# Gate and up weights in two pieces each, and a down projection that writes output rows directly, at the end of a memory-bound decode kernel

## The chip, the cores and the metric

The kernel runs on one core of one Trainium2 chip. The metric is the device time of one execution in microseconds (us); I quote medians of several runs. In the profile, PE is the tensor engine's matmuls, PEld its weight loads, DVE the vector engine, ACT the scalar engine, SP the engine that issues the large DMAs, and PEclk the tensor engine's granted clock as a share of full speed. "L748" is a line of that kernel's source; the same statement has other line numbers in other kernels.

## The reference, cut to what matters

Four sequences, one new token each (B = 4, model width D = 512): attention over a cache of 8192 keys for 32 heads, then a gated feed-forward block (F = 1792).

```
h   = x + attention(layernorm(x), k_cache, v_cache, wq, wo)
n   = layernorm(h)
g   = n @ w_gate                 # [4, 512] @ [512, 1792]
u   = n @ w_up                   # [4, 512] @ [512, 1792]
out = h + (sigmoid(g) * u) @ w_down     # [4, 1792] @ [1792, 512]
```

The two caches are 537 MB in bfloat16; the three weights of the feed-forward block are 1.8 MB each.

## The kernel before

The caches stream through a ring of four buffers for some 1250 us. The change touches only what follows: the loads of the last weights, and the feed-forward block. There, `NFT = 14` tiles of F, `NDC = 4` chunks of D. Activations are kept transposed (the feature on the 128 partitions, 4 columns for the batch), so each weight block of 128 x 128 is the stationary operand and only 4 columns are streamed through it:

```
WD_PARTS = [(0, 7), (7, 12), (12, NFT)]      # w_down arrives in three pieces
...
def pe_gu(e, wv, bk):                        # gate, then up
    mm = None
    for t in range(NFT):
        for c in range(NDC):
            mm = e.matmul(bk[:, B * t:B * t + B], wv[:, c, t:F:NFT],
                          hnT[:, B * c:B * c + B], start=(c == 0), stop=(c == NDC - 1))
    return mm
p_g = P("pe", lambda e: pe_gu(e, wg_v, bS[0]), [d_hn, dma_of[("wg", 0)][0]])
p_u = P("pe", lambda e: pe_gu(e, wu_v, bS[1]), [dma_of[("wu", 0)][0]])
a_sig = ...                                  # sg_sb = sigmoid(gate)
d_hh = ...                                   # hh_sb = sg_sb * up
...
        for c in range(NDC):                 # down, for t in the piece
            mm = e.matmul(bH[:, B * c:B * c + B], wd_v[:, t, 128 * c:128 * (c + 1)],
                          hh_sb[:, B * t:B * t + B], ...)
...
d_o = ...                                    # oT = h + down, rearranged to (b c) columns
p_o = P("pe", lambda e: e.matmul(bP[0][0:NB, 0:128], oT[:, :], ident[:, :], ...), ...)   # transpose
o0 = P("dve", lambda e: e.tensor_copy(o_sb[:, :], bP[0][0:NB, 0:128]), [p_o])
# then one DMA to out
```

In the first argument of `P` stands the engine, in the last list what the operation waits for.

## Time and profile before

| | before |
|---|---|
| time, median of 6 runs | 1287.07 us (1286.68 to 1287.3) |
| profiled span | 1285.0 us |
| moved from HBM | 550.77 MB at 429 GB/s |
| chain that ended last | 84% DMA |

These are lines of the page of the kernel before (busy tenths in 40 slices; then HBM traffic; then the chain that ended last, by engine).

```profile
DMA  9999999999999999999999999999999999999998
HBM read 550.77 MB, written 0.00 MB: 429 GB/s over the span
DMA 84%; PE 13%; DVE 2%; issue 0%; SPq 0%; DVEq 0%
```

The DMA engines are busy from first to last. This change moves no byte less and does not touch the loads of the caches, so the time before the last weights arrive should stay as it is; only what happens between the last landings and the end can move. So this is the timeline of the end, with the columns: start, duration, engine, line, operation, output<-inputs, shapes, count, and in brackets how long the engine was idle just before and what ended that.

```profile
1267.83 1.44 PE L715 MATMUL PS<-A_sb,kT 128*128 128x4 bf16 x48 [0.22 <-DMA kT<-in_A_wo_dram]
...
1271.48 0.17 DVE L739 TENSOR_TENSOR hnT<-hc,tst 128x16 bf16<-128x16 f32 x1
...
1272.49 3.49 PE L748 MATMUL PS<-hnT,ring 128*128 128x4 bf16 x56 [2.11 <-DMA ring<-in_B_w_gate_dram]
1276.83 3.52 PE L748 MATMUL PS<-hnT,ring 128*128 128x4 bf16 x56 [0.85 <-DMA ring<-in_B_w_up_dram]
1280.46 0.21 DVE L754 TENSOR_TENSOR hh_sb<-sg_sb,PS 128x56 bf16<-128x56 f32 x1 [8.80 <-PE PS L748]
...
1280.73 1.66 PE L762 MATMUL PS<-hh_sb,ring 128*128 128x4 bf16 x56 [0.38 <-DVE hh_sb L754]
1282.42 0.19 DVE L768 TENSOR_TENSOR oT<-h,PS 128x16 bf16<-128x16 f32 x1 [1.75 <-PE PS L762]
...
1282.67 0.28 PE L771 MATMUL PS<-ident,oT 128*16 128x128 bf16 x1 [0.28 <-DVE oT L768]
1282.98 0.28 DVE L773 CAST o_sb<-PS 16x128 bf16<-16x128 f32 x1 [0.37 <-PE PS L771]
```

Three things are to be seen. Gate waits for its whole weight, although its input was ready 0.8 us sooner, and up waits 0.85 us for its own. A gate or up matmul takes 63 ns (3.52 us / 56), a down matmul only 29.6 ns (1.66 us / 56), both at the same granted clock of 0.50, as the windows view says (the down stretch; its limits and length, then busy time and number of instructions of PE, PEld, DVE, ACT and POOL, then PEclk, the DMA share and GB/s):

```profile
1280.73:1282.39 1.66, 1.65 (x56) 1.56 (x56) 0.00 (x0) 0.00 (x0) 0.00 (x0) 0.50 0.00 0
```

And after down there are three more steps, with hand-offs between engines, before the output DMA.

The last weight pieces land close behind. From the DMA issues of the same kernel (KB, median us from issue to landing; the issues started at 1244.6, 1263.4 and 1265.3) the three pieces of the down weight land at about 1279.0, 1280.5 and 1281.2:

```profile
ring<-in_B_w_down_dram SPq DMA_DIRECT2D x1, 896.0 KB, 34.3
ring<-in_B_w_down_dram SPq DMA_DIRECT2D x1, 640.0 KB, 17.1
ring<-in_B_w_down_dram SPq DMA_DIRECT2D x1, 256.0 KB, 15.9
```

### The profile page before, as it was taken

To read this page: it belongs to the slowest core of one execution; us is meant where nothing else is said; L and a number is where in the kernel's file an instruction comes from. 1 tells how busy PE (TensorE), PEld (TensorE's weight loads), DVE (VectorE), ACT (ScalarE), POOL (GpSimd) and SP (SyncE) were. 2 spreads that over 40 slices of the span, in tenths; PEclk is the share of its full clock that TensorE was granted. 3 is DMA by queue.
4 is the path that set the end of the run, shared out by engine and by line. 5 is a ranking of instruction groups with operands and counts; after the bars stand their busy time and mean duration, and the time that the engine had idled before them with its cause. 6 is when DMAs were issued, how large, how long until landed. Compare 5 with 4: busy or idle time off the path is not lost.

```text
span 1285.0 us, 11783 instructions
## 1 busy us (share of the span) xinstructions
PE 499.6 (39%) x4851; PEld 187.0 (15%) x4851; DVE 634.8 (49%) x659; ACT 77.2 (6%) x150; POOL 8.3 (1%) x23
## 2 busy tenths in 40 slices
PE   3434344334244244333434343253342442343445
PEld 1011111111011011111111111010110111111114
DVE  4974634635545545535536445445445446355300
ACT  2010100001010010100101000010100101000011
POOL 2000000000000000000000000000000000000000
PEclk9995565565665665565665665655665656655665
DMA  9999999999999999999999999999999999999998
GB/s 406 429 431 430 433 431 432 431 432 433 429 432 432 430 431 431 432 431 433 430 433 430 432 431 430 433 429 435 429 435 429 436 428 432 432 429 433 430 435 341
DMA packets 20405, 550.95 MB, mean 429 GB/s; under 512 B 2212, under 2 KB 2216, under 8 KB 3624
## 3 DMA queue, kind: packets, MB, share of 16 engines
q1 hardware_dynamic: 20384, 550.78, 99.7%
q8 instruction: 8, 0.13, 0.0%
q14 instruction: 5, 0.04, 0.0%
q10 hardware_dynamic: 8, 0.00, 0.0%
HBM read 550.77 MB, written 0.00 MB: 429 GB/s over the span
## 4 chain that ended last, share of the span: by engine, by line
DMA 84%; PE 13%; DVE 2%; issue 0%; SPq 0%; DVEq 0%
DMA ring<-in_A_v_cache_dram 79%; PE PS L544 8%; PE PS L522 4%; DMA ring<-in_B_w_up_dram 3%; DMA ring<-in_A_k_cache_dram 2%; DVE kT L497 1%; DMA ring<-in_A_wq_dram 1%; PE PS L575 1%; PE PS L427 0%; PE PS L748 0%; DVE Lq L470 0%; DVE ring L444 0%; PE PS L454 0%; PE PS L762 0%; SPq L325 0%
## 5 line engine op out<-in xcount | busy, mean ns | idle before, releaser
L497 DVE STREAM_TRANSPOSE kT<-ring 128x1024 uint32<-128x1024 uint32 x512 | 588.4, 1209 | 475.1 <-DMA ring<-in_A_k_cache_dram 474.9
L522 PE MATMUL PS<-kT,Lqg 128*32 128x512 bf16 x2048 | 242.2, 621 | 569.4 <-DVE kT L497 569.4
L544 PE MATMUL PS<-ring,PTz 128*32 128x512 bf16 x2048 | 216.1, 568 | 192.1 <-DMA ring<-in_A_v_cache_dram 192.1
L522 PEld LDWEIGHTS PS<-kT,Lqg 128*32 128x32 bf16 x2048 | 69.5, 135 | 700.5 <-DVE kT L497 445.5
L544 PEld LDWEIGHTS PS<-ring,PTz 128*32 128x32 bf16 x2048 | 64.6, 128 | 311.6 <-DMA ring<-in_A_v_cache_dram 183.3
L606 DVE STREAM_TRANSPOSE Et<-Ep 128x512 bf16<-128x512 bf16 x16 | 11.4, 712 | 96.4 <-ACT Ep L601 96.4
L579 ACT ACTIVATE negm<-PS 128x1 f32<-128x1 f32 x16 | 2.7, 171 | 669.3 <-PE PS L575 669.3
L616 ACT ACTIVATE PTz<-Et 64x512 bf16<-64x512 bf16 x32 | 34.0, 1062 | 13.6 <-DVE Et L606 13.2
L645 ACT ACTIVATE A_sb<-PS 32x32 bf16<-32x32 f32 x16 | 3.7, 231 | 479.5 <-PE PS L643 479.5
L621 DVE TENSOR_SCALAR Zs<-PS,rinv 128x512 f32<-128x512 f32 x16 | 11.6, 723 | 27.6 <-PE PS L544 27.6
L629 PE MATMUL PS<-SelZ,Zs 128*128 128x8 f32 x128 | 18.6, 272 | 0.9 <-DVE Zs L621 0.9
L629 PEld LDWEIGHTS PS<-SelZ,Zs 128*128 128x128 f32 x128 | 17.1, 208 | 10.6 <-issue 10.6
L558 DVE TENSOR_REDUCE mx<-PS 128x1 f32<-128x512 f32 x16 | 10.5, 657 | 4.2 <-PE PS L522 4.2
L581 ACT ACTIVATE E_sb<-PS,negm 128x512 bf16<-128x512 f32 x16 | 11.0, 688 | 0.7 <-ACT negm L579 0.3
L601 ACT ACTIVATE Ep<-PS 128x512 bf16<-128x512 f32 x16 | 9.6, 597 | 11.1 <-PE PS L597 11.1
L586 PEld LDWEIGHTS PS<-sig,Gsum 128*128 128x128 f32 x32 | 7.8, 305 | 13.1 <-issue 13.1
L586 PE MATMUL PS<-sig,Gsum 128*128 128x1 f32 x32 | 9.2, 356 | 0.0
L575 PEld LDWEIGHTS PS<-onesf,rowx 1*128 1x128 f32 x32 | 6.9, 267 | 12.8 <-issue 12.8
L444 DVE CAST ring<-PS 128x512 bf16<-128x512 f32 x4 | 2.5, 683 | 12.2 <-PE PS L427 12.2
L575 PE MATMUL PS<-onesf,rowx 1*128 1x1 f32 x32 | 8.2, 324 | 0.0
L748 PE MATMUL PS<-hnT,ring 128*128 128x4 bf16 x112 | 7.0, 199 | 3.0 <-DMA ring<-in_B_w_gate_dram 2.1
L635 DVE TENSOR_TENSOR OD<-PS,SelD 128x32 bf16<-128x32 f32 x16 | 2.5, 157 | 10.3 <-PE PS L629 10.3
(87 smaller groups left out, 98.2 us busy)
## 6 DMA issues: line engine op xcount, KB each, us to landing
ring<-in_A_k_cache_dram SPq DMA_DIRECT2D x64, 4096.0 KB, 29.5
ring<-in_A_v_cache_dram SPq DMA_DIRECT2D x64, 4096.0 KB, 33.6
ring<-in_A_wq_dram SPq DMA_DIRECT2D x1, 4096.0 KB, 12.5
kT<-in_A_wo_dram SPq DMA_DIRECT2D x1, 2560.0 KB, 21.4
ring<-in_B_w_gate_dram SPq DMA_DIRECT2D x1, 1792.0 KB, 28.7
ring<-in_B_w_up_dram SPq DMA_DIRECT2D x1, 1792.0 KB, 32.7
kT<-in_A_wo_dram SPq DMA_DIRECT2D x1, 1536.0 KB, 24.6
ring<-in_B_w_down_dram SPq DMA_DIRECT2D x1, 896.0 KB, 34.3
```

Source lines behind the costliest of these rows:

```text
L497: return e.transpose(kT[:, buf, i * q:(i + 1) * q].bitcast(U32), ringv(src)[:, base + i * q:base + (i + 1) * q].bitcast(U32))
L522: mm = e.matmul(bS[g % 2][32 * j:32 * (j + 1), :], Lqg[:, g % 2, l0:l0 + 32], rhs, start=(s % GS == 0 and v == 0), stop=(s % GS == GS - 1 ...
L544: mm = e.matmul(bO[g % 2][32 * rq:32 * (rq + 1), :], PTz[:, g % 2, l0:l0 + 32], ringv(slot)[:, r0 * 128:(r0 + 4) * 128], start=(s % GS == ...
L558: mx_of[g] = P("dve", lambda e: e.tensor_reduce(mx[:, :], bS[g % 2][:, :], AX.X, ALU.max), [sc_of[g * GS + GS - 1], p1_of.get(g - 1)], kin ...
L575: p2_of[g] = P("pe", lambda e: e.matmul(bX[:, 0:1], rowx[0:1, :], onesf[0:1, 0:1], start=True, stop=True), [d2b_of[g], c_ones], kind="p2")
L581: exp_of[g] = P("act", lambda e: e.activation(E_sb[:, :], bS[g % 2][:, :], ACT.Exp, bias=negm[:, 0:1], scale=SCALE, accum_out=sig[:, 0:1]) ...
L586: L_of[g] = P("pe", lambda e: e.matmul(bX[:, 0:1], Gsum[:, :], sig[:, 0:1], start=True, stop=True), [exp_of[g], a1_of[g], d_g], kind="L")
L601: epc_of[g] = P("act", lambda e: e.activation(Ep[:, :], bP[0][:, :], ACT.Copy), [pt_of[g], et_of.get(g - 1)], kind="epc")
L606: et_of[g] = P("dve", lambda e: e.transpose(Et[:, :], Ep[:, :]), [epc_of[g]] + list(ptc_of.get(g - 1, ())), kind="et")
L616: return e.activation(dst, src, ACT.Copy)
L621: z_of[g] = P("dve", lambda e: e.tensor_scalar(Zs[:, :], bO[g % 2][:, :], rinv[:, g % 2:g % 2 + 1], None, op0=ALU.mult), [pv_of[g * GS + G ...
L629: mm = e.matmul(bP[1][:, 0:8], Zs[:, 128 * r:128 * (r + 1)], SelZ[:, r, :], start=(r == 0), stop=(r == 3))
```

## The change

Its intent: let gate and up start on the first half of their weights, and let the down projection leave its result in the layout of the output, so that the residual add and the transposing matmul after it fall away. The core of the diff (the split of the two loads, with a semaphore for each half, and the zeroing of `hhz` are cut):

```diff
-        def pe_gu(e, wv, bk):
+        def pe_gu(e, wv, bk, i):
             mm = None
-            for t in range(NFT):
-                for c in range(NDC):
-                    mm = e.matmul(bk[:, B * t:B * t + B], wv[:, c, t:F:NFT],
-                                  hnT[:, B * c:B * c + B], start=(c == 0), stop=(c == NDC - 1))
+            for c in range(2 * i, 2 * i + 2):
+                for t in range(NFT):
+                    mm = e.matmul(bk[:, B * t:B * t + B], wv[:, c, t:F:NFT], hnT[:, B * c:B * c + B],
+                                  start=(c == 0 and t == 0), stop=(c == NDC - 1 and t == NFT - 1), ...)
             return mm
 ...
-        d_hh = ...(hh_sb[:, :], sg_sb[:, :], bS[1][:, 0:NFT * B], ALU.mult)
+        d_hh = ...(hhz[:, :, 3:3 + NB:4], sg_sb ..., bS[1] ..., ALU.mult)
 ...
+        o_ps = bP[0][0:NB, 0:128]
+        p_h = P("pe", lambda e: e.matmul(o_ps, hb[:, :], identf[:, :], start=True, stop=False, ...), ...)
 ...
-                        mm = e.matmul(bH[:, B * c:B * c + B], wd_v[:, t, 128 * c:128 * (c + 1)],
-                                      hh_sb[:, B * t:B * t + B], ...)
+                        mm = e.matmul(o_ps, hhz[:, t, 3 - c:3 - c + NB], wd_v[:, t, 128 * c:128 * (c + 1)],
+                                      start=False, ...)
 ...
-        d_o = ...      # residual add
-        p_o = ...      # transposing matmul
-        o0 = P("dve", lambda e: e.tensor_copy(o_sb[:, :], bP[0][0:NB, 0:128]), [p_o])
+        o0 = P("dve", lambda e: e.tensor_copy(o_sb[:, :], o_ps), [p_d[-1]])
```

How the shifted slices work: for each tile `t`, `hhz` has 20 columns, all zero but columns 3, 7, 11 and 15, which hold the four sequences. The slice of 16 columns that starts at `3 - c` has sequence b in its column 4b + c. With it as the stationary operand and a down block as the streamed one, the product lands in output row 4b + c, which is where chunk c of sequence b belongs; the other 12 rows get zero added. The roles have swapped: 16 columns are loaded, and the 128 columns of the weight are streamed. `p_h` starts the sum with the residual.

More of the change, by code (lines that the diff above doesn't have):

```diff
@@ L246, in bass_sequential_preLN__mha_block_cached__glu_gated_glu__decode_kernel @@
         hc = SB("hc", [128, NDC * B], FP32)
+        hb = SB("hb", [128, NDC * B], FP32)
         hnT = SB("hnT", [128, NDC * B], BF16)
         sg_sb = SB("sg_sb", [128, NFT * B], FP32)
-        hh_sb = SB("hh_sb", [128, NFT * B], BF16)
-        oT = SB("oT", [128, B * NDC], BF16)
+        hhz = SB("hhz", [128, NFT, 20], BF16)
         o_sb = SB("o_sb", [B * NDC, 128], BF16)
@@ L267, in bass_sequential_preLN__mha_block_cached__glu_gated_glu__decode_kernel @@
         s_slot = [SEM(f"s_slot{i}") for i in range(NS)]
-        s_piece = [SEM(f"s_piece{i}") for i in range(7)]
+        s_piece = [SEM(f"s_piece{i}") for i in range(9)]
         def ringv(slot):
@@ L333, in f @@
                                            B_w_down.rearrange("(p t) f -> p t f", p=128)[:, t0:t1, :]
-                                           ).then_inc(s_piece[3 + i], 16)
-                    ops.append((f, s_piece[3 + i], 16))
-                return ops
-            if kind == "wu":
-                sem, val = s_piece[6], 16
-            else:
-                uses[slot] += 1
-                sem, val = s_slot[slot], 16 * uses[slot]
+                                           ).then_inc(s_piece[2 + i], 16)
+                    ops.append((f, s_piece[2 + i], 16))
+                return ops
+            if kind in ("wg", "wu"):
+                ops = []
+                for i in range(2):
+                    wv, src, sem = (wg_v, B_w_gate, s_piece[5 + i]) if kind == "wg" else (wu_v, B_w_up, s_piece[7 + i])
+                    def f(e, i=i, wv=wv, src=src, sem=sem):
+                        return e.dma_start(wv[:, 2 * i:2 * i + 2, :],
+                                           src.rearrange("(c p) f -> p c f", p=128)[:, 2 * i:2 * i + 2, :]).then_inc(sem, 16)
+                    ops.append((f, sem, 16))
+                return ops
+            uses[slot] += 1
+            sem, val = s_slot[slot], 16 * uses[slot]
             if kind == "k":
@@ L345, in load @@
                 dst, src = ringv(slot), kv_src(t, A_v_cache)
-            elif kind == "wq":
+            else:
                 dst, src = wq_v, A_wq.rearrange("(p c) f -> p c f", p=128)
-            elif kind == "wg":
-                dst, src = wg_v, B_w_gate.rearrange("(c p) f -> p c f", p=128)
-            else:
-                dst, src = wu_v, B_w_up.rearrange("(c p) f -> p c f", p=128)
             return [(lambda e: e.dma_start(dst, src).then_inc(sem, 16), sem, val)]
@@ L382, in bass_sequential_preLN__mha_block_cached__glu_gated_glu__decode_kernel @@
                        [zs4])
+        zhh = pool(lambda e: e.memset(hhz[:, :, :], 0.0))
         zif = pool(lambda e: e.memset(identf[:, :], 0.0))
@@ L741, in bass_sequential_preLN__mha_block_cached__glu_gated_glu__decode_kernel @@
                                                   mean_b(20), ALU.mult), [d_rs, d_hc])
+        d_hb = P("dve", lambda e: e.tensor_copy(hb[:, :].rearrange("p (b c) -> p c b", c=NDC),
+                                                h2[:, 0, :].rearrange("p (c b) -> p c b", c=NDC)), [d_h])
         P("act", lambda e: e.activation(lnst[0:B, 10:11], tst[0:B, 12:13], ACT.Sigmoid), [a_sq])
-        def pe_gu(e, wv, bk):
+        def pe_gu(e, wv, bk, i):
             mm = None
-            for t in range(NFT):
-                for c in range(NDC):
-                    mm = e.matmul(bk[:, B * t:B * t + B], wv[:, c, t:F:NFT],
-                                  hnT[:, B * c:B * c + B], start=(c == 0), stop=(c == NDC - 1))
-            return mm
-        p_g = P("pe", lambda e: pe_gu(e, wg_v, bS[0]), [d_hn, dma_of[("wg", 0)][0]])
-        p_u = P("pe", lambda e: pe_gu(e, wu_v, bS[1]), [dma_of[("wu", 0)][0]])
-        a_sig = P("act", lambda e: e.activation(sg_sb[:, :], bS[0][:, 0:NFT * B], ACT.Sigmoid), [p_g])
-        d_hh = P("dve", lambda e: e.tensor_tensor(hh_sb[:, :], sg_sb[:, :], bS[1][:, 0:NFT * B], ALU.mult), [a_sig, p_u])
+            for c in range(2 * i, 2 * i + 2):
+                for t in range(NFT):
+                    mm = e.matmul(bk[:, B * t:B * t + B], wv[:, c, t:F:NFT], hnT[:, B * c:B * c + B],
+                                  start=(c == 0 and t == 0), stop=(c == NDC - 1 and t == NFT - 1), skip_group_check=True)
+            return mm
+        p_g, p_u = [], []
+        for ps, kind, wv, bk in ((p_g, "wg", wg_v, bS[0]), (p_u, "wu", wu_v, bS[1])):
+            for i in range(2):
+                ps.append(P("pe", lambda e, wv=wv, bk=bk, i=i: pe_gu(e, wv, bk, i), [d_hn, dma_of[(kind, 0)][i]]))
+        a_sig = P("act", lambda e: e.activation(sg_sb[:, :], bS[0][:, 0:NFT * B], ACT.Sigmoid), [p_g[1]])
+        d_hh = P("dve", lambda e: e.tensor_tensor(hhz[:, :, 3:3 + NB:4], sg_sb[:, :].rearrange("p (t b) -> p t b", b=B),
+                                                  bS[1][:, 0:NFT * B].rearrange("p (t b) -> p t b", b=B), ALU.mult),
+                 [a_sig, p_u[1], zhh])
+        o_ps = bP[0][0:NB, 0:128]
+        p_h = P("pe", lambda e: e.matmul(o_ps, hb[:, :], identf[:, :], start=True, stop=False, skip_group_check=True),
+                [d_hb, c_identf, epc_of[gl]])
         p_d = []
@@ L761, in pe_down @@
                     for c in range(NDC):
-                        mm = e.matmul(bH[:, B * c:B * c + B], wd_v[:, t, 128 * c:128 * (c + 1)],
-                                      hh_sb[:, B * t:B * t + B], start=(t == 0 and c == 0),
-                                      stop=(t == NFT - 1 and c == NDC - 1), skip_group_check=True)
-                return mm
-            p_d.append(P("pe", pe_down, [d_hh, dma_of[("wd", 0)][i], d_h]))
-        d_o = P("dve", lambda e: e.tensor_tensor(oT[:, :].rearrange("p (b c) -> p c b", c=NDC),
-                                                 h2[:, 0, :].rearrange("p (c b) -> p c b", c=NDC),
-                                                 bH[:, 0:NB].rearrange("p (c b) -> p c b", c=NDC), ALU.add), [p_d[-1]])
-        p_o = P("pe", lambda e: e.matmul(bP[0][0:NB, 0:128], oT[:, :], ident[:, :], start=True, stop=True),
-                [d_o, epc_of[gl]])
-        o0 = P("dve", lambda e: e.tensor_copy(o_sb[:, :], bP[0][0:NB, 0:128]), [p_o])
+                        mm = e.matmul(o_ps, hhz[:, t, 3 - c:3 - c + NB], wd_v[:, t, 128 * c:128 * (c + 1)],
+                                      start=False, stop=(t == NFT - 1 and c == NDC - 1), skip_group_check=True)
+                return mm
+            p_d.append(P("pe", pe_down, [d_hh, dma_of[("wd", 0)][i]]))
+        o0 = P("dve", lambda e: e.tensor_copy(o_sb[:, :], o_ps), [p_d[-1]])
         consumed[("wg", 0)] = consumed[("wu", 0)] = consumed[("wd", 0)] = p_d[-1]
```

## The prediction

Written before the changed kernel was built or run.

> **What bounds the kernel now.** HBM traffic. The page shows 550.77 MB at 429 GB/s over a span of 1285.0 us, DMA busy in tenths 9 in nearly every slice, and 84% of the chain that ended last is DMA. The change moves no byte less, so only the tail after the last big loads can move. In the timeline the tail is: output projection done 1269.3; normalised hidden state ready 1271.65; gate matmuls 1272.49 to 1275.98 (56, about 63 ns each; they waited for the whole gate weight until 1272.3); 0.85 us wait for the up weight (landed 1276.8); up matmuls 1276.83 to 1280.35; product 0.21 us; down matmuls 1280.73 to 1282.39 (56, 29.6 ns each); residual add 0.19, transposing matmul 0.28, copy 0.28 (ends 1283.26); output DMA and end, 1.75 us. The down weight's three pieces land at about 1278.9, 1280.4 and 1281.2.
>
> **What the change removes and adds.**
> 1. Gate and up in halves over d outermost. Same weight views, same 112 matmuls, so I keep 63 ns each. Gate half 0 should land near 1270.1, so gate starts on the hidden state at about 1271.9, not 1272.5; up half 0 should land near 1274.5, so the 0.85 us wait goes. Four halves of 1.76 us run back to back: up ends near 1278.9 instead of 1280.35. Gain 1.4 us, all on the chain.
> 2. Residual add and transposing matmul after down go (about 0.55 us with their hand-offs). The residual now enters as an fp32 matmul queued between up and down. Its time is partly hidden behind the product; I charge 0.1 us.
> 3. The down projection swaps roles. Before, 128 columns of weight were loaded and 4 columns streamed: 29.6 ns. Now 16 columns are loaded and 128 streamed. In this trace 16 attention matmuls of 512 columns, four at a time on four column groups, take 1.75 us: 0.85 ns per column, so 128 columns cost 109 ns. The windows view shows the granted clock at 0.50 for the whole tail. 56 x 109 = 6.1 us, against 1.66 us. [...] the clock here indeed rises at 1223.0 and 1233.2, after windows full of 512-column matmuls, but not after the dense 4-column gate and up matmuls. So I expect the clock to rise somewhere inside the new down stage, phase unknown: an estimated 4.4 to 6.7 us, centre 5.5. Loss about 3.8 us.
>
> **Sum.** -1.4 - 0.55 + 0.1 + 3.8 = about +1.9; allowing that the clock may rise earlier than I think, I predict 1288.6 us, with 1287.2 to 1289.9 as the 8-in-10 range. Chances: faster by over 2% 0.01, within 2% 0.98, slower by over 2% 0.01.
>
> **What would show each step right or wrong.** Step 1: the timeline has 112 gate and up matmuls without the 0.85 us gap, ending near 1278.9 (shifted to the same end of attention). Step 2: no DVE and PE step between down and the output copy. Step 3: the down group of 56 matmuls takes over 4.4 us, starts 100 to 125 ns apart while the windows view shows clock 0.50, about half that after it rises. DMA rate before the tail unchanged.
>
> **What would make it wrong.** The clock rises already during gate and up (now 7 us unbroken): then down takes about 3.2 us and the change gains half a microsecond. The 16-column weight loads do not hide behind the streams: down near 7 us. Smaller gate and up DMAs delay the issue or landing of the down weight.

The sum: -1.4 - 0.55 + 0.1 + 3.8 came to +1.95 us over 1287.07 us, and with 0.4 us taken off for an earlier rise of the clock to 1288.6 us. What stands on the trace of before is the estimate of 109 ns for a matmul at clock 0.50, from attention matmuls, and that the clock rose at 1223.0 and 1233.2 us, after stretches in which PE was busy for 3.41 of 3.41 and 3.40 of 3.40 us (1219.59 to 1223.00 and 1229.8 to 1233.2). That it would rise inside the new down stage, with the range of 4.4 to 6.7 us and the centre of 5.5, was the author's estimate, as were the 3.2 and 7 us under what would make it wrong; the loss of 3.8 us is that centre less 1.66.

## More of the kernel before

Note `t:F:NFT` in gate and up: the 128 columns of a weight block are every 14th column.

## The result, and the profile after

| | before | after |
|---|---|---|
| median of 6 runs | 1287.07 us | 1288.41 us |
| range | 1286.68 to 1287.3 | 1287.67 to 1288.78 |
| profiled span | 1285.0 us | 1286.5 us |

The ratio is 1.001 (95% interval 0.9997 to 1.0023). The interval does not exclude 1, but the two sets of runs do not overlap, and the experiments below repeat the difference.

The page after shows the same DMA load:

```profile
DMA  9999999999999999999999999999999999999997
HBM read 550.77 MB, written 0.00 MB: 428 GB/s over the span
```

The timeline of the end, after, in the same columns:

```profile
1267.65 1.44 PE L719 MATMUL PS<-A_sb,kT 128*128 128x4 bf16 x48 [0.19 <-DMA kT<-in_A_wo_dram]
...
1271.54 6.98 PE L754 MATMUL PS<-hnT,ring 128*128 128x4 bf16 x112 [1.34 <-DVE hnT L743]
...
1278.45 0.61 PE L768 MATMUL PS<-identf,hb 128*16 128x128 f32 x2
1278.61 0.31 DVE L762 TENSOR_TENSOR hhz<-sg_sb,PS 128x56 bf16<-128x56 f32 x1 [7.04 <-issue]
...
1278.98 5.47 PE L776 MATMUL PS<-ring,hhz 128*16 128x128 bf16 x56
1284.48 0.28 DVE L780 CAST o_sb<-PS 16x128 bf16<-16x128 f32 x1 [5.56 <-PE PS L776]
```

The output projection (first line) starts 0.18 us earlier here than in the profile of before. That is scatter of the run (in the seven profiles with halved loads it starts between 1267.65 and 1268.31), so I take the shift out. Then the two profiles differ by four terms:

| step | before | after | difference, shift taken out |
|---|---|---|---|
| end of up (1276.83 + 3.52; 1271.54 + 6.98) | 1280.35 | 1278.52 | -1.65 |
| end of up to start of down | 0.38 | 0.46 | +0.08 |
| down | 1.66 | 5.47 | +3.81 |
| end of down to end of output copy | 0.87 | 0.31 | -0.56 |
| sum | | | +1.68 |

The spans differ by 1.5 us, and 1.68 with the shift taken out, so the terms account for all of it. Gate and up now run as one block of 112 matmuls with no wait for a DMA, and the two steps after down are gone. The price is the down group.

The windows view shows why it costs that much. Each line is one stretch of the profile after, with the columns given above. The first stretch lies within gate and up, the second within down, the third in the last part of down.

```profile
1273.40:1276.70 3.30, 3.30 (x57) 3.28 (x56) 0.00 (x0) 0.22 (x1) 0.00 (x0) 0.50 1.06 428
1280.20:1283.50 3.30, 3.30 (x34) 3.30 (x32) 0.00 (x0) 0.00 (x0) 0.00 (x0) 0.50 0.03 9
1283.60:1284.40 0.80, 0.80 (x15) 0.66 (x12) 0.00 (x0) 0.00 (x0) 0.00 (x0) 1.00 0.00 0
```

In the trace 44 down matmuls start while the clock is granted at 0.50, 106 to 107 ns apart (the first two 70 ns). The clock rises to 1.00 at 1283.57, and from there the starts are 55 to 56 ns apart. It is 128 columns before the rise and 128 after it, so the same matmul took 1.9 times as long at the clock of 0.50 as at 1.00. That the streamed columns set the pace, and not another cost of each matmul, is tested below (e5: 53 to 54 ns with 64 columns).

### The profile page after: what moved, and what is told of

Read it like the earlier page. It is cut to its first block, busy times and chain, and to the rows that moved or that the text cites. A ratio compares the mean times of both kernels' runs of the same rounds, so it can differ in the third digit from the quotient of the medians.

```text
span 1286.5 us, 11788 instructions
## 1 busy us (share of the span) xinstructions
PE 501.1 (39%) x4852; PEld 189.8 (15%) x4852; DVE 638.0 (50%) x659; ACT 77.3 (6%) x150; POOL 8.4 (1%) x24
## 4 chain that ended last, share of the span: by engine, by line
DMA 84%; PE 14%; DVE 2%; issue 0%; SPq 0%; ACT 0%
DMA ring<-in_A_v_cache_dram 79%; PE PS L548 8%; PE PS L526 4%; DMA ring<-in_A_k_cache_dram 2%; DMA kT<-in_A_wo_dram 2%; DVE kT L501 1%; DMA ring<-in_A_wq_dram 1%; PE PS L754 1%; PE PS L579 1%; PE PS L776 0%; PE PS L431 0%; DVE Lq L474 0%; DVE ring L448 0%; PE PS L458 0%; PE PS L719 0%
## 5 line engine op out<-in xcount | busy, mean ns | idle before, releaser
L601 PE MATMUL PS<-E_sb,Sel 128*32 128x512 bf16 x64 | 6.9, 421 | 2.2 <-ACT E_sb L585 1.9
## 6 DMA issues: line engine op xcount, KB each, us to landing
ring<-in_A_k_cache_dram SPq DMA_DIRECT2D x64, 4096.0 KB, 29.5
```

## The experiments

Theory A: the change is two opposed parts. The halves gain time, the row-wise down loses more, and what it loses is streamed columns at half clock. Theory B, the rival: the halves themselves cost (more and smaller DMAs, later landings), or the price of the row-wise down lies elsewhere (per matmul, in its weight load from the padded tile, in the added residual matmul). The first four kernels ran on one chip with five rounds and share nine runs of the kernel before: 1287.02 us (1286.79 to 1287.41). The last three ran together, on another chip, with three rounds: before 1286.82 us (1286.76 to 1287.29). Across the two sets only the difference to each set's own before should be compared.

| run | median us | range |
|---|---|---|
| before (first four) | 1287.02 | 1286.79 to 1287.41 |
| e1 halves only | 1286.10 | 1286.01 to 1286.43 |
| e2 rows only | 1289.96 | 1289.26 to 1290.62 |
| e3 changed kernel again | 1288.29 | 1287.61 to 1289.07 |
| e4 column groups | 1285.79 | 1285.72 to 1285.95 |
| before (last three) | 1286.82 | 1286.76 to 1287.29 |
| e5 half the columns (wrong result) | 1286.36 | 1286.17 to 1286.38 |
| e6 no residual (wrong result) | 1288.47 | 1287.93 to 1288.88 |
| e7 neighbouring columns (wrong result) | 1285.99 | 1285.74 to 1286.38 |

### e1: the halves alone

The changed kernel, with the product, the down projection and everything after it put back as before.

```diff
-                        mm = e.matmul(o_ps, hhz[:, t, 3 - c:3 - c + NB], wd_v[:, t, 128 * c:128 * (c + 1)], start=False, ...)
+                        mm = e.matmul(bH[:, B * c:B * c + B], wd_v[:, t, 128 * c:128 * (c + 1)],
+                                      hh_sb[:, B * t:B * t + B], ...)
+        d_o = ...    # residual add, as before
+        p_o = ...    # transposing matmul, as before
```

> Gate and up in halves, down projection as before. Theory A (the two parts of the change oppose each other, the halves gain and the row-wise down costs): up ends about 1.8 us earlier than before, but down then waits for its own last weight piece, which lands about 3.9 us before the end of the span of before; so the gain is capped at about 0.9 to 1.0 us, 1286.1 against 1287.05. The chain should name the down weight's DMA. Theory B (the smaller DMAs are what costs, later landings or later issue): no gain or a loss, and gate, up or down weights land later than before relative to the output weight.

Measured: 1286.10 us, 0.92 under before (ratio 0.9993, interval 0.9979 to 1.0007, which does not exclude 1; but the slowest run of e1 is under the fastest of before). The halves gain, and theory B's first form falls: the last pieces of the gate, up and down weights land within 0.15 us of where those of before land (the second piece of the down weight at 1280.6 here, at 1280.5 before). The PE part of the timeline of e1:

```profile
1271.86 6.94 PE L751 MATMUL PS<-hnT,ring 128*128 128x4 bf16 x112 [1.34 <-DVE hnT L742]
...
1279.24 0.89 PE L767 MATMUL PS<-hh_sb,ring 128*128 128x4 bf16 x28 [0.44 <-DVE hh_sb L759]
...
1280.67 0.97 PE L767 MATMUL PS<-hh_sb,ring 128*128 128x4 bf16 x28 [0.54 <-DMA ring<-in_B_w_down_dram]
```

and the head of its chain of work that ended last (start, us, what):

```profile
1263.43 17.20 DMA ring<-in_B_w_down_dram
1280.62 0.04 issue
1280.67 0.98 PE PS L767 x28
```

Up ends more than 1.5 us sooner, but down then stops in the middle, 0.54 us, for its own weight. In the kernel before it never waited there. The gain is capped by a DMA that was hidden until now.

### e2: the row-wise down alone

The changed kernel, with gate and up and their loads put back as before (one DMA and one wait each).

```diff
-        p_g, p_u = [], []
-        for ps, kind, wv, bk in ...:
-            for i in range(2):
-                ps.append(P("pe", ... pe_gu(e, wv, bk, i), [d_hn, dma_of[(kind, 0)][i]]))
+        p_g = P("pe", lambda e: pe_gu(e, wg_v, bS[0]), [d_hn, dma_of[("wg", 0)][0]])
+        p_u = P("pe", lambda e: pe_gu(e, wu_v, bS[1]), [dma_of[("wu", 0)][0]])
```

> Gate and up as before, down projection as rows of shifted slices. Theory A: the down group takes 4.4 to 6.0 us instead of 1.66 (106 ns a matmul at clock 0.50, 55.7 ns after it rises), less 0.55 us for the removed add and transposing matmul: +2.2 to +3.8 us, centre +3.1, so about 1290.2, and a spread between runs of over 1 us because the rise falls at another moment each time. Theory B: the row-wise down costs nothing by itself, time within 0.5 us of before.

Measured: 1289.96 us, 2.94 over before (ratio 1.0024, interval 1.0011 to 1.0038, which excludes 1). The spread of five runs is 1.36 us, against 0.62 us of nine runs before. In its profile down takes 4.62 us, less than in the changed kernel, because the clock rose sooner: after 27 matmuls instead of 44. This is the down group of e2, then the two stretches before and after the rise (windows view, columns as above):

```profile
1280.75 4.62 PE L771 MATMUL PS<-ring,hhz 128*16 128x128 bf16 x56
```

```profile
1280.20:1283.50 3.30, 3.30 (x31) 2.88 (x31) 0.31 (x1) 0.00 (x0) 0.00 (x0) 0.50 0.03 11
1283.60:1285.30 1.70, 1.70 (x31) 1.59 (x29) 0.00 (x0) 0.00 (x0) 0.00 (x0) 1.00 0.00 0
```

### e3: the changed kernel again

No edit; run beside e1, e2 and e4.

> The changed kernel unaltered, on the same chip as the others. Theory A: +1.3 us against before (1288.4), with a run-to-run spread near 1 us; the gain of the halves beside the row-wise down (this run against rows only) is the full 1.7 to 1.9 us, more than the halves gain alone, since here down no longer waits for its weights. Theory B: this run is slower than or equal to rows only.

Measured: 1288.29 us, 1.27 over before, with a spread of 1.46 us. In this profile down takes 5.58 us and the clock rises after about 46 of its 56 matmuls. Against e2 the halves now gain 1.67 us (just under the 1.7 that I expected), against 0.92 us alone. The two parts do not add: slow rows give the down weight time to land, so with them all of the halves' gain counts (in the profile after the second piece lands at 1280.4, and the first matmul that needs it starts at 1281.9). Nowhere in the profile of e3 does down wait for a DMA:

```profile
1279.59 5.58 PE L776 MATMUL PS<-ring,hhz 128*16 128x128 bf16 x56
```

The 1.67 us rests on two medians of five runs each, with ranges of 1.36 and 1.46 us, so it is uncertain by some tenths. The two profiles alone do not show it: e2's is of its fastest run and e3's of its slowest, and their spans are 0.19 us apart.

### e4: the four column blocks at once

If what costs is columns streamed one after another, then streams that run side by side should win it back. Each column block c of the down weight gets a 32-column group of the array, with 4 stationary columns taken from the unpadded product. Output chunk c lies on partitions 32c to 32c + 3. The residual comes as one matmul over all 128 partitions, and four small copies, two each on DVE and ACT, bring the chunks together.

```diff
-                        mm = e.matmul(o_ps, hhz[:, t, 3 - c:3 - c + NB], wd_v[:, t, 128 * c:128 * (c + 1)],
-                                      start=False, stop=(t == NFT - 1 and c == NDC - 1), ...)
+                        mm = e.matmul(bP[0][32 * c:32 * c + B, 0:128], hh_sb[:, B * t:B * t + B],
+                                      wd_v[:, t, 128 * c:128 * (c + 1)], start=False, stop=(t == NFT - 1),
+                                      tile_position=(0, 32 * c), ...)
 ...
-        o0 = P("dve", lambda e: e.tensor_copy(o_sb[:, :], o_ps), [p_d[-1]])
+        o0 = []      # for each c, on DVE or ACT:
+            src, dst = bP[0][32 * c:32 * c + B, 0:128], o_sb[:, 128 * c:128 * (c + 1)]
```

> As the changed kernel, but the four column blocks of the down weight stream at once, each in its own 32-column group of the array with 4 stationary columns; the result is copied by four small copies on two engines. Theory A (what costs is columns streamed one after another at half clock): the four streams share their time, the group needs about 1.5 us of stream instead of 5.4 and becomes bound by the landing of the last down weight piece; down ends about 0.35 us after that landing, the output copies end 0.4 us later, total about 1.2 us under before: 1285.8. Rival (each matmul costs about 100 ns whatever runs beside it, through its weight load or its operands): down stays at 5 us or more and the time near 1288.4.

Measured: 1285.79 us, correct, 1.23 under before and the best of all kernels here. Its slowest run (1285.95) is under the fastest of before (1286.79); the interval of the ratio (0.9977 to 1.0004) is wider than that and does not exclude 1. The timeline of e4 for down and the copies:

```profile
1279.24 0.92 PE L773 MATMUL PS<-ring,hh_sb 128*4 128x128 bf16 x28
...
1280.57 1.01 PE L773 MATMUL PS<-ring,hh_sb 128*4 128x128 bf16 x28 [0.41 <-DMA ring<-in_B_w_down_dram]
...
1281.63 0.56 ACT L782 ACTIVATE o_sb<-PS 4x128 bf16<-4x128 f32 x2 [6.17 <-PE PS L773]
1281.63 0.60 DVE L782 CAST o_sb<-PS 4x128 bf16<-4x128 f32 x2 [2.63 <-PE PS L773]
```

Four matmuls start within 14 ns of each other, and the next four 106 to 107 ns after them (the first group 61 ns), with the clock at 0.50 throughout: four streams in the time of one. The 56 matmuls need 2.3 us, instead of 5.5, with the waits for the weight: 0.41 us for its second piece, and some 0.2 us more, before the last eight matmuls, for its third, which lands at 1281.15. The copies take 0.60 us, longer than the 0.4 us that I had allowed.

### e5: half the columns

```diff
-                        mm = e.matmul(o_ps, hhz[:, t, 3 - c:3 - c + NB], wd_v[:, t, 128 * c:128 * (c + 1)],
+                        mm = e.matmul(o_ps[:, 0:64], hhz[:, t, 3 - c:3 - c + NB], wd_v[:, t, 128 * c:128 * c + 64],
```

> Wrong result on purpose: the changed kernel with only 64 of the 128 columns of each down weight block streamed; the same 56 matmuls, the same 16-column weight loads. Theory A (a matmul costs its streamed columns at the granted clock): starts about 53 ns apart at clock 0.50, down about 3.0 us, no or almost no part of it at the full clock, time about 1286.0, under the kernel before. Rival (the number of matmuls, their weight loads from the padded tile or the accumulation into one bank set the pace): still about 106 ns apart and about 1288.4.

Measured: starts 53 to 54 ns apart (the first two 36 ns), all of them at clock 0.50, and this down group:

```profile
1279.29 3.16 PE L776 MATMUL PS<-ring,hhz 128*16 128x64 bf16 x56
```

The same 56 matmuls with the same 16-column weight loads into the same bank start half as far apart when they stream half the columns. The rival (a price per matmul) falls. The time is 1286.36 us, where I had written 1286.0. In its profile gate starts at 1271.87, 0.33 us later than in the changed kernel's, though nothing ahead of it was edited; such scatter of the part before the tail is as large as the miss.

### e6: no residual matmul

The matmul `p_h` is taken out, and the first down matmul starts the sum; one of the waits of `p_h` moves to down.

```diff
-        p_h = P("pe", lambda e: e.matmul(o_ps, hb[:, :], identf[:, :], start=True, stop=False, ...), ...)
 ...
-                                      start=False, stop=...
+                                      start=(t == 0 and c == 0), stop=...
```

> Wrong result on purpose: the changed kernel without the fp32 matmul that adds the residual. Theory A (it runs while the product is being formed on VectorE, so it is hidden): down still starts about 0.45 us after up ends, time within 0.3 us of the changed kernel (1288.3), which its run-to-run spread hides. Rival (it stands in front of down): down starts 0.3 us or more sooner after up.

Measured: down starts 0.46 us after the end of up (1279.03 to 1279.49), exactly as with the residual matmul (1278.52 to 1278.98):

```profile
1272.07 6.96 PE L754 MATMUL PS<-hnT,ring 128*128 128x4 bf16 x112 [1.34 <-DVE hnT L743]
...
1279.49 5.49 PE L774 MATMUL PS<-ring,hhz 128*16 128x128 bf16 x56 [0.46 <-DVE hhz L762]
```

The time is 1288.47 us, 1.65 over its own before, against 1.27 to 1.34 with the residual matmul; with ranges near 1 us, and on another chip, that says nothing about 0.1 us, and the timeline decides. The fp32 matmul is hidden: the tensor engine would wait for the product anyway.

### e7: what bounds the column groups

The column-group kernel, with gate and up taking 128 neighbouring columns instead of every 14th, which should make those matmuls cheaper (before, the down matmuls with neighbouring columns took 29.6 ns each, gate and up with every 14th column 63 ns).

```diff
-                    mm = e.matmul(bk[:, B * t:B * t + B], wv[:, c, t:F:NFT], hnT[:, B * c:B * c + B],
+                    mm = e.matmul(bk[:, B * t:B * t + B], wv[:, c, 128 * t:128 * (t + 1)], hnT[:, B * c:B * c + B],
```

> Wrong result on purpose: the column-group version with each gate and up weight block taken as 128 neighbouring columns instead of every 14th. Expected: these 112 matmuls take about 30 ns each instead of 62, as the down matmuls of before do, so up ends about 0.9 us after its last half lands (1277.7 instead of 1278.6). If the landing of the last down weight piece bounds the column-group version, the time stays at 1285.8 within 0.2 us although the tensor engine has 1 us less to do; if the tensor engine bounds it, 0.5 us or more is gained.

Measured: gate takes 1.65 us instead of 3.5 (29.5 ns a matmul instead of 62 to 63), and up's last half follows its landing by 0.95 us. The time is 1285.99 us (1285.74 to 1286.38), 0.83 under its own before, where e4 was 1.23 under its own: no gain. The PE timeline shows that each saved stretch became a wait for a DMA:

```profile
1271.88 1.65 PE L754 MATMUL PS<-hnT,ring 128*128 128x4 bf16 x56 [1.34 <-DVE hnT L743]
...
1275.20 0.91 PE L754 MATMUL PS<-hnT,ring 128*128 128x4 bf16 x28 [1.68 <-DMA ring<-in_B_w_up_dram]
...
1277.45 0.91 PE L754 MATMUL PS<-hnT,ring 128*128 128x4 bf16 x28 [1.34 <-DMA ring<-in_B_w_up_dram]
...
1281.18 1.02 PE L773 MATMUL PS<-ring,hh_sb 128*4 128x128 bf16 x28 [0.54 <-DMA ring<-in_B_w_down_dram]
```

So the end of the column-group version is bound by the landing of the down weight: the last eight matmuls start 0.04 us after its third piece lands (1281.78), as in e4. In this one profile, of the slowest run, the pieces from up on landed 0.6 us later than in e4; why is open, and it blurs the comparison of the times by that much.

## Why the prediction was right, point by point

The prediction was 1288.6 us with a range of 1287.2 to 1289.9; measured 1288.41. The mechanism was right; that the number came within 0.2 us is partly luck. The predicted steps add up to +1.95 us, and 0.4 was taken off for a clock that might rise earlier. It did not: down took 5.47 us where the centre was 5.5. What made the loss smaller was a gain of the halves 0.25 us larger than predicted (+1.68 in the profiles with the shift taken out, +1.34 in the medians).

- **"Only the tail can move."** Right: the same bytes at 428 and 429 GB/s, and the four terms of the tail add up to the difference of the spans, with the shift of 0.18 us taken out.
- **Step 1, the halves: predicted 1.4 us, measured 1.65.** The gate matmuls started 0.77 us earlier instead of 0.6 (shift taken out), because the hand-off from the hidden state took 0.06 us, not the quarter of a microsecond that I allowed; the rest of the wait for up fell away as said, and the 62 to 63 ns per matmul held. Two predicted landings were close: 1270.1 and 1274.5 for the first halves, against 1269.9 and 1274.4 in the trace. The prediction said the gain lies wholly on the chain; that holds beside slow rows, but e1 shows that it does not hold by itself (0.92 us), for a reason that the prediction did not see: the down weight's own landing.
- **Step 2, the removed steps: predicted 0.55 us, measured 0.56.** The 0.1 us that I charged for the residual matmul was the wrong cause: e6 shows it hidden. There is a cost of about that size, but it is in the product, which takes 0.31 us instead of 0.21 in the changed kernel; it writes every fourth column of a padded tile there. That the stride is the reason was not tested alone; e4 and e1, which write without it, have 0.21.
- **Step 3, the swapped roles: predicted 3.8 us of loss, measured 3.81.** A matmul costs 106 ns where I had 109, read from attention matmuls of another shape. The clock rose inside the down group, as expected. The four profiles with all 128 columns streamed one after another (after, e2, e3, e6) give 5.47, 4.62, 5.58 and 5.49 us, all inside the predicted 4.4 to 6.7; the upper end, for weight loads that do not hide, was not needed. That the changed kernel's profile fell on the centre is chance: in e2 the clock rose earlier within down, and 4.62 us would have made the loss 2.96 us.
- **The three dangers.** The clock did not rise during gate and up: 3.3 us of those matmuls without a gap leave it at 0.50. The prediction read this from the profile before, which shows it only in part: between the lines of the clock's 3.41 us grid (see below) PE was busy there for 2.57 us (1274.20 to 1277.62, because of the wait for up) and 3.03 us (1277.62 to 1281.03), and the 60 rises of the clock in that trace follow stretches of the grid with 2.73 us or more. The profile after shows it with PE busy for the whole of a stretch (1273.33 to 1276.75). The same 3.3 us of 128-column matmuls (1280.2 to 1283.5) are followed by a clock of 1.00; whether it is the few columns or something else about the gate and up matmuls that left the clock at 0.50 was not tested. The 16-column weight loads do hide behind the streams: with half the columns the starts come 53 ns apart instead of 106 (e5), while the profile there gives a load a median of 118 ns (138 in the profile after), so the loads overlap the streams. The down weight did not land later.

The spread fits in part. Kernels with a long row-wise down have ranges of 0.95 to 1.46 us (four sets of runs); the others have 0.21 to 0.64. In the traces of before and after every change of the clock (121 and 125 of them) lies within 0.001 us of a grid of 3.413 us. In these traces the grid is not tied to the kernel's start: reckoned from the first instruction, its first line falls at 1.03 us in the profile before and at 0.16 us in the profile after. In e3, the same kernel as after, the clock rose near 1284.4 us instead of 1283.57 (an estimate: 46 starts 106 to 107 ns apart, from 1279.59 on). A rise that comes a microsecond later costs about half a microsecond: from the start of down it came after 2.82 us in e2 and after 4.59 us in the profile after, and down took 4.62 and 5.47 us. The grid is not the only source of the spread: the profiles after and e3 have spans 0.74 us apart, of which 0.61 us are there when down starts (1278.98 and 1279.59), and only 0.11 us come from down. How much each adds over many runs is not shown.

## What to carry to other kernels

When a matmul has one thin side, count the columns that are streamed and not the instructions: loading the wide weight and streaming 4 columns cost 29.6 ns here, loading the thin side and streaming 128 columns cost 106 ns (53 ns for 64 columns, e5) at the same granted clock of 0.50, and it saved only 0.56 us of steps behind it. If the thin side must be stationary, put the blocks side by side in column groups, where four streams took the time of one (106 to 107 ns, e4). And when a wait is taken away at the end of a memory-bound kernel, look up what lands next: nearly half of a gain vanished here into a DMA that was hidden before (0.92 us of 1.65 were left), and two changes that look independent may share it.
